# Two routed expert layers on one core: where GpSimd rounds the second weights, and how the second layer's token lists are made

## The chip, the cores and the metric

The kernel runs on one core of a Trainium2 chip. The metric is the device time of one execution in microseconds (us); three executions of the kernel before took 448.25, 448.32 and 449.85 us, median 448.32 us. In the profile TensorE's matmuls are called PE and its weight loads PEld, VectorE is DVE, ScalarE is ACT, GpSimd is POOL, and SyncE, which only issues transfers here, is SP.

## The reference

```python
attn_out = _attn_ref(x, state)            # 4 x 8 x (512 + 32) x 64
x = attn_out.transpose(0, 2, 1, 3).reshape(2176, 512)
x = _moe_ref(x, w_gate, w1, w2, capacity) # 8 experts, capacity 576, top 1
return _moe2_ref(x, w_gate, w1, w2)       # 8 experts, no capacity

# an expert layer, in short:
expert = argmax(x @ w_gate); gate = softmax(x @ w_gate)[expert]
h = relu(x_e @ w1[e])                     # 512 -> 1024
y = h @ w2[e]                             # 1024 -> 512
out[token] = gate * y                     # zero for a token beyond the capacity
```

## The kernel before

The attention comes first, then the two expert layers, called layer 0 and layer 1 (`L` in the code). Within a layer the tokens of each expert are taken in groups of 512, a "stage" each (`stage(L, k)`, L1472, and `tail`, L1527): tokens are gathered by an indirect DMA, turned by TensorE, multiplied by the first weights, passed through the relu and multiplied by the second weights. Each float32 product is made of three products of rounded parts, high by high, high by low and low by high. So every weight has to be split. The high part is a cast on ACT. The low part is weight minus high part, one subtraction on GpSimd or VectorE. Here three stages run in layer 0 and three in layer 1.

**Order of a stage.** A stage is 16 products in a fixed order (`ORDER`, L1455): eight first products (`m1_quad`, L1159, three steps of four matmuls each) and eight second products (`m2_quad`, L1171, four steps of three matmuls each), the second product of a chunk one place behind the first product of the next. These are 56 steps, numbered from 0. Every engine gets its instructions in the order in which the program is written. After each step the program puts in other work (`Part.__call__`, L1504): first one advance of a foreground generator, then the events listed for that step number, then some advances of background work (`tick`). `yield` in a generator means "the rest goes behind the next step". What the foreground generator has not done by the end of its part of the stage (in layer 0's stages 1 and 2 that is step 31) is written out at once, with no product between.

**Splitting the second weights.** `wsplit(1, c, on)` (L275) splits a quarter `c` of the second weights: ACT casts 128x1024 elements (L280), and POOL, or DVE where `on` says 0, subtracts (L281). Four quarters are done behind the steps `SPLIT2`. Steps 1, 3, 5, 7 (`SPLITB`) split the second half of the first weights the same way in tiles of 128x512 (L1385). A quarter `c` is first needed by the second product `2c`, that is at steps 6, 20, 34 and 48. Behind the last split stands `load_next`, which has SP load the next stage's second weights into the same raw buffers.

**Routing of layer 1.** While layer 0's stages 1 and 2 and layer 1's stage 0 run, the outputs of the stage before are routed for layer 1. `Logits` turns 128-token tiles on TensorE and multiplies them by the gate weights (L1221, L1231, L1232). When the last tile's logits are there, `behind` (L1245) runs as the foreground generator: the expert by maximum and comparisons on DVE (`argmax_onehot`, L284, which yields after every third operation), then the "rank products" on TensorE that count earlier tokens of the same expert (L1260 to L1264), then place and gate of each token on DVE (`slots`, `gate_of`), the row stores by indirect DMA on POOL (`stores`, L1193), and then for each tile two one-hot matrices on DVE (`enlist`, L339 and L341) and two "list products" on TensorE that write token numbers into expert lists in PSUM (`enlist_mm`, L347). The one-hots have two buffers, used in turn, and the list product of a tile is written two steps behind its one-hots. In layer 0's stage 2 there follow `set_apart` (L366) and `early_list` (L432), which copies the lists out of PSUM, multiplies them once more (L442) and works out the row numbers for layer 1's first gather (L415). In layer 1's stage 0, `plan_lists` (L575) does the same for all lists (L582, L413), and `planned` (L1594) waits for the plan, has POOL convert it (L1596) and has SP start loading the weights of layer 1's stage 1.

Of the kernel before, what the change touches and what calls it, by code (L numbers as in the profile page):

```python
# [13 lines left out]
F16 = mybir.dt.float16  # L14
# [6 lines left out]
P = 128  # L21
# [13 lines left out]
QT = NEARLY  # L35
NJ = -(-(NTOK + NROWS - 1) // (QT * P)) * QT
NK = E * NJ
# [21 lines left out]
LISTS = (30, 32, 34, 36)  # L59
CUT = (2, 9, 11)  # L60
SPLITA = (0, 2, 4, 6)
SPLITB = (1, 3, 5, 7)
SPLIT2 = (0, 8, 14, 20)
TQ, TQ2, FG, STEP = (3, 2, 1, 3)
PLANNED, READY, GET = ((20, 29), 37, 0)
GAP = 2
HINT0 = 30
TURNS0 = ((0, 1, 2), (4, 5, 6), (6, 7, 8))
ON = ((1, 1, 1, 1), (1, 1, 1, 1), (0, 0, 0, 0), (0, 0, 0), (1, 1, 1, 1))
TURNS = ((6, 7, 8), (8, 10, 12), (12, 13, 14))  # L70
ALL = (ET.Pool, ET.Activation, ET.PE, ET.DVE, ET.SP)
WHY = "the value is a count worked out on the chip within these bounds"
# [3 lines left out]
def moe_kernel(ctx: ExitStack, tc: tile.TileContext, x, state, wg1, w1a, w2a, cap, wg2, w1b, w2b, out):  # L76
# [14 lines left out]
    lists = listp[0:KH, 0:2]  # L91
# [58 lines left out]
    def run_all(g):  # L150
        for _ in g:
            clock[0] += 1
# [119 lines left out]
            k = t.shape[1]  # L272
            SP.dma_start(out=t, in_=src[:, c * k:(c + 1) * k, :])

    def wsplit(which, c, on=ON[2], quick=False):  # L275
        t, h, l = raw[0][which][c], wset[which][0][c], wset[which][1][c]
        if quick:
            DVE.tensor_copy(h, t)
        else:
            ACT.copy(h, t)  # L280
        (POOL if on[c] else DVE).tensor_tensor(out=l, in0=t, in1=h.bitcast(F32), op=ALU.subtract)  # L281
# [55 lines left out]
    def enlist(oc, ov, np_, pp, ek, code, res):  # L337

        DVE.tensor_scalar(oc[0:np_], iofm[0:np_], ek[0:np_], None, op0=ALU.is_equal)  # L339
        yield  # L340
        DVE.tensor_scalar(ov[0:np_], iofb[0:np_], pp[0:np_], code[0:np_], op0=ALU.is_equal, op1=ALU.mult)  # L341
        yield
        res.append((np_, oc, ov))

    def enlist_mm(np_, oc, ov):
        for h in range(2):
            PE.matmul(lists[:, h], oc[0:np_, h * KH:(h + 1) * KH], ov[0:np_], start=False, stop=True, skip_group_check=True)  # L347
# [17 lines left out]
    def set_apart(pool):  # L365

        run = runs_[1]
        t = pool.tile([P, E], F32, tag="sa", name="sa")
        DVE.tensor_scalar(t, run, -1.0, float(NROWS), op0=ALU.mult, op1=ALU.add)
        yield  # L370
        DVE.tensor_scalar(t, t, 0.0, None, op0=ALU.max)
        yield
        DVE.tensor_tensor(out=t, in0=t, in1=first, op=ALU.mult)
        yield
        DVE.tensor_tensor(out=run, in0=run, in1=t, op=ALU.add)
        yield
# [742 lines left out]
    gy = wk2.tile([P, QT + 2], F32, name="gy")  # L1119
    meta = wk2.tile([P, NY, 3], F32, name="meta")  # L1120
    dsti = wk2.tile([P, NY], I32, name="dsti")
    oc2 = wk2.tile([P, 2, NK], F16, name="oc2")
    ov2 = wk2.tile([P, 2, P], F16, name="ov2")
    qs = ctx.enter_context(tc.tile_pool(name="qs", bufs=1, space=bass.MemoryType.PSUM))
    ph = [qs.tile([P, 512], F32, name=f"ph{i}") for i in range(2)]
    py = [qs.tile([P, 512], F32, name=f"py{i}") for i in range(QT)]
# [115 lines left out]
                ev += [(t, lambda i=2 * j + k: self.turn(i)) for k, t in enumerate(ts)]  # L1242
            return ev

    def behind(lt, counted=None):  # L1245


        n, y0, lg = lt.n, lt.y0, lt.lg
        pool = Sized(n)
        m = meta[:, y0:y0 + n]  # L1250
        while lt.done < n:
            yield
        oh = pool.tile([P, n, E], BF16, "oh", "oh2")
        mv = []
        DVE.tensor_copy(dsti[:, y0:y0 + n], m[:, :, 2])
        yield from every(STEP, argmax_onehot(pool, lg, n, m[:, :, 1], oh, mv))

        w = n * E
        ohv = oh.rearrange("p n e -> p (n e)")
        PE.matmul(pyv[:, 0:w], upper, ohv, start=True, stop=True)  # L1260
        for i in range(1, n):
            PE.matmul(pyv[:, i * E:w], ones, ohv[:, 0:(n - i) * E], start=False, stop=True, skip_group_check=True)
        for i in range(n):
            PE.matmul(pyv[:, w:w + E], ones, ohv[:, i * E:(i + 1) * E], start=(i == 0), stop=(i == n - 1))  # L1264
        run = runs_[1]
        pre = pool.tile([P, n, E], F32, "pre", "pre2")
        res = []

        def places():
            DVE.tensor_tensor(out=pre, in0=bc(run[:, None, :], [P, n, E]), in1=pyv[:, 0:w].rearrange("p (n e) -> p n e", n=n), op=ALU.add)  # L1270
            DVE.tensor_tensor(out=run, in0=run, in1=pyv[:, w:w + E], op=ALU.add)
            if counted is not None:
                counted()
            yield
            yield from slots(pool, oh, mv[1], pre, n, res)

        def gates():
            yield from gate_of(pool, lg, mv[0], n, gy[:, 0:n])
            DVE.tensor_copy(ysb[:, y0:y0 + n, DM], gy[:, 0:n])
            stores(0, range(y0, y0 + n))  # L1280

        yield from every(2 * STEP, abreast(places(), gates()))
        todo = []
        for i in range(n):
            run_all(enlist(oc2[:, i % 2], ov2[:, i % 2], P, res[0][:, i:i + 1], res[1][:, i:i + 1], m[:, i, 0:1], todo))
            for _ in range(GAP):
                yield
            if i:
                enlist_mm(*todo.pop(0))
        enlist_mm(*todo.pop(0))  # L1290
        yield

    def nothing(m):

# [65 lines left out]
    def load_next(L, k, *which):  # L1360

        if k < ML:
            n = load_reg(L, 0, spo, ML)
            with tc.If(n > k) as cmp:
                e = load_reg(L, QEXP + k, spo, E - 1)
                for i in which:
                    wload(0, i, W[L][i], e)
            if L == 0 and k > 2:
                with cmp.Else():
                    run_all(load_first(1, which))  # L1370
        elif L == 0:
            run_all(load_first(1, which))
# [20 lines left out]
    def at(places, f, *args):  # L1393
        return [(p, lambda c=c: f(*args, c)) for c, p in enumerate(places)]
# [63 lines left out]
    def hint(label, hints):  # L1458

        with tc.block():  # L1460
            for h, engs in hints:
                tc.mark_branch_hint_location(label, hint=h, engines=engs)
# [8 lines left out]

    def stage(L, k, ev=(), ticks=0, fg=()):  # L1472

        lists = [at(SPLIT2, lambda c: wsplit(1, c, ON[4 if L or k else 2])), ev]
        if L or k:
            lists.append(at(SPLITB, split1, 1))
        if k:
            lists.append([(SPLITB[-1] + 1, lambda: load_next(L, k + 1, 0)), (SPLIT2[-1] + 1, lambda: load_next(L, k + 1, 1))])
        st = Stage(lists)
        DVE.tensor_copy(mcur, cols(L, k))  # L1480
        DVE.tensor_copy(gq[0], gq[1])
        if k == 0:
            st.common(CUT[2], ticks, fg)
            return st
        s = 2 * (k - 1)
        y = 0 if k % 2 == 0 else NY - 1

        def small1(kind):
            yield from one(L, kind - 1, s, y)
            load_small(L, s + 1)  # L1490
            get_small(L, s + 1)

        def small2(kind):
            yield from one(L, kind - 1, s + 1, NY - 2)
            if k < NA:
                load_small(L, 2 * k)
                get_small(L, 2 * k)

        if L == 0:
            if k == 1:  # L1500
                fill_out()
            nothing(meta[:, y:y + 1])
        if k <= NA:
            st.variants(CUT[0], kd_[s], small1)  # L1504
        st.common(CUT[1], 0, fg)
        if L == 0:
            nothing(meta[:, NY - 2:NY - 1])
        if k <= NA:
            st.variants(CUT[2], kd_[s + 1], small2, f"end{L}{k}", hints(L, k))
        else:  # L1510
            st.common(CUT[2])
        return st

    def beside(L, k, lt):

        if L == 0:
            yield from behind(lt)
            if k == 1:
                yield from popular(rp, 1, runs_[1], most)
            if k == 2:  # L1520
                yield from apart()

    def apart():
        yield from set_apart(rp)
        yield from early_list(rp, 1)
# [66 lines left out]
    def planned(L):  # L1592
        while "nr" not in rt:
            assert bgq  # L1594
            tick()
        POOL.tensor_copy(ri[L], rt.pop("nr"))  # L1596
        load_next(L, 1, 0)
# [18 lines left out]
        x_quad(t, ysb[:, 1 + t], py[t], False)  # L1616
    reads[3][2]()
    bgq.append(chain(fills(2, 3), route(1, B - 1, (3, 0, 0, 0), False, (plan_runs(rp, 0), chain(positions(0), until_placed(), positions(1)))), enlist_all()))
    st = stage(0, 0, at(LISTS, list_product) + [(LISTS[-1] + 1, listed), (PLANNED[0], lambda: planned(0)), (SPLIT2[-1] + 1, lambda: load_next(0, 1, 1)), (READY, room), (HINT0, lambda: hint("end00", (("LikelyTaken", ALL),)))], TQ)
    ready(0)  # L1620
    list_clear()
    deeper(st, 0, 0)
# [2 lines left out]
    def routed():  # L1625
        yield from behind(lt, lambda: bgq.append(plan_runs(rp, 1)))
        bgq.append(plan_lists(rp, 1))

    lt = Logits(QT + 2, 0)
    st = stage(1, 0, lt.events(TURNS0) + [(PLANNED[1], lambda: planned(1)), (PLANNED[1] + 1, lambda: load_next(1, 1, 1))], TQ2, routed())  # L1630
    ready(1)
    deeper(st, 1, 0)

# [37 lines left out]
```

## Time and profile before

| | us | share of the span |
|---|---|---|
| median of three runs | 448.32 | |
| profiled execution | 452.34 | |
| its span, first to last instruction | 450.5 | |
| PE busy | 418.6 | 93% |
| PEld busy | 301.6 | 67% |
| DVE busy | 186.3 | 41% |
| POOL busy | 184.8 | 41% |
| ACT busy | 161.3 | 36% |
| mean granted TensorE clock | 0.987 of full | |

The shares are averages over a span in which PE nearly always has work. A row of a timeline reads: start in us, length in us, engine, line, operation, output <- inputs, shape, count, and in brackets how long the engine was idle before it and what ended that wait. Neighbouring matmuls overlap in it, so what a step costs is read from one start to the next and not from the lengths.

Layer 0's stage 1 starts at about 116.4 us of the span, its stage 2 at 188.1, layer 1's stage 0 at 260.7 and its stage 1 at 315.6.

### The profile page before, as it was taken

To read this page: it belongs to the slowest core of one execution; us is meant where nothing else is said; L and a number is where in the kernel's file an instruction comes from. 1 tells how busy PE (TensorE), PEld (TensorE's weight loads), DVE (VectorE), ACT (ScalarE), POOL (GpSimd) and SP (SyncE) were. 2 spreads that over 40 slices of the span, in tenths; PEclk is the share of its full clock that TensorE was granted. 3 is DMA by queue.
4 is the path that set the end of the run, shared out by engine and by line. 5 is a ranking of instruction groups with operands and counts; after the bars stand their busy time and mean duration, and the time that the engine had idled before them with its cause. 6 is when DMAs were issued, how large, how long until landed. Compare 5 with 4: busy or idle time off the path is not lost. (4 is left out here: it accounts for less than half of the span.)

```text
span 450.5 us, 8000 instructions
## 1 busy us (share of the span) xinstructions
PE 418.6 (93%) x2746; PEld 301.6 (67%) x2746; DVE 186.3 (41%) x576; ACT 161.3 (36%) x291; POOL 184.8 (41%) x166
## 2 busy tenths in 40 slices
PE   7899879999998999999988999999989999999991
PEld 4676658867646847757754876788547848768780
DVE  7988898943314511512650336854210101411111
ACT  4587553203443214545202464114313214452110
POOL 7343300017245454064442544475717207677003
PEclk9899999999999999999989999999999999999997
DMA  7965999599999478089331200239989668210002
GB/s 218 304 169 130 353 176 182 98 341 342 384 402 371 177 226 331 3 300 378 120 98 51 73 0 4 101 135 388 387 291 328 228 226 277 75 49 7 9 0 93
DMA packets 48229, 88.13 MB, mean 196 GB/s; under 512 B 8592, under 2 KB 23440, under 8 KB 48144
## 3 DMA queue, kind: packets, MB, share of 16 engines
q1 hardware_dynamic: 43344, 72.43, 50.5%
q0 software_dynamic: 4800, 14.71, 9.3%
q8 instruction: 36, 0.59, 0.6%
q14 instruction: 49, 0.40, 0.3%
HBM read 66.65 MB, written 21.52 MB: 196 GB/s over the span
## 5 line engine op out<-in xcount | busy, mean ns | idle before, releaser
L1157 DVE SCALAR_TENSOR_TENSOR hTl<-ph,hTh 128x512 fp32r<-128x512 f32 x48 | 33.2, 691 | 199.4 <-ACT hTh L1156 184.0
L1175 PE MATMUL py<-w1h,hTh 128*128 128x512 f32 x192 | 81.4, 424 | 0.0
L1175 PE MATMUL py<-w1h,hTl 128*128 128x512 f32 x192 | 75.4, 393 | 0.0
L1175 PE MATMUL py<-w1l,hTh 128*128 128x512 f32 x192 | 75.1, 391 | 0.0
L1156 ACT ACTIVATE hTh<-ph 128x512 fp32r<-128x512 f32 x48 | 28.7, 599 | 128.9 <-PE ph L1165 74.3
L1385 POOL TENSOR_TENSOR w0l<-raw,w0h 128x512 fp32r<-128x512 f32 x40 | 50.9, 1291 | 36.7 <-ACT w0h L1384 34.5
L281 POOL TENSOR_TENSOR w1l<-raw,w1h 128x1024 fp32r<-128x1024 f32 x20 | 47.8, 2397 | 41.3 <-ACT w1h L280 41.2
L1165 PE MATMUL ph<-xTh,w0h 128*128 128x512 f32 x192 | 54.1, 403 | 4.4 <-PEq L1578 2.5
L1165 PE MATMUL ph<-xTl,w0h 128*128 128x512 f32 x192 | 55.6, 411 | 0.1
L1165 PE MATMUL ph<-xTh,w0l 128*128 128x512 f32 x192 | 54.9, 408 | 0.0
L1165 PEld LDWEIGHTS ph<-xTh,w0h 128*128 128x128 f32 x192 | 35.2, 188 | 13.8 <-issue 4.3
L1165 PEld LDWEIGHTS ph<-xTl,w0h 128*128 128x128 f32 x192 | 35.2, 188 | 13.8 <-issue 6.1
L1175 PEld LDWEIGHTS py<-w1h,hTh 128*128 128x128 f32 x192 | 36.1, 188 | 9.5 <-issue 3.4
L1165 PEld LDWEIGHTS ph<-xTh,w0l 128*128 128x128 f32 x192 | 35.3, 191 | 9.8 <-issue 2.5
L1175 PEld LDWEIGHTS py<-w1h,hTl 128*128 128x128 f32 x192 | 36.0, 188 | 8.1
L1175 PEld LDWEIGHTS py<-w1l,hTh 128*128 128x128 f32 x192 | 36.3, 189 | 6.6 <-issue 1.0
L1193 POOL DMA_INDIRECT out_dram<-ysb,dsti x15 | 14.9, 993 | 60.3 <-ACT ysb L1183 53.3
L1193 POOL DMA_INDIRECT yrows<-ysb,dsti x16 | 16.0, 1000 | 27.4 <-DVE oc L339 8.0
L1384 ACT CAST w0h<-raw 128x512 fp32r<-128x512 f32 x40 | 23.8, 617 | 5.4 <-DMA raw<-in_moe_w_dram 5.2
L280 ACT CAST w1h<-raw 128x1024 fp32r<-128x1024 f32 x24 | 25.1, 1046 | 0.1
L977 PE MATMUL pav<-vg,e1T 128*128 128x264 f32 x56 | 16.6, 421 | 1.3 <-ACT lgx L982 1.3
L1324 PE MATMUL pyT<-raw,xTf 128*32 128x256 f32 (+1 forms) x144 | 16.8, 454 | 0.0
(355 smaller groups left out, 555.0 us busy)
## 6 DMA issues: line engine op xcount, KB each, us to landing
raw<-in_moe_w_dram SPq DMA_DIRECT2D x104, 512.0 KB
out_dram<-zb SPq DMA_DIRECT2D x2, 2176.0 KB
xb<-in_x_dram SPq DMA_DIRECT2D x6, 512.0 KB
xrows<-xr SPq DMA_DIRECT2D x8, 256.0 KB
yrows<-zb SPq DMA_DIRECT2D x3, 514.0 KB
yrows<-zb SPq DMA_DIRECT2D x3, 512.0 KB
xb<-in_x_dram SPq DMA_DIRECT2D x4, 256.0 KB
xrows<-ysb SPq DMA_DIRECT2D x4, 256.0 KB
```

What stands on the lines that cost most here:

```text
L280: ACT.copy(h, t)
L281: (POOL if on[c] else DVE).tensor_tensor(out=l, in0=t, in1=h.bitcast(F32), op=ALU.subtract)
L977: PE.matmul(pv[:, a, 0:GW], e1_[b][:, r % 2, a, r // 2], vg[:, b, a], start=True, stop=True)
L1156: ACT.activation(out=hTh[:, c % 2], in_=p, func=AF.Relu)
L1157: DVE.scalar_tensor_tensor(out=hTl[:, c % 2], in0=p, scalar=0.0, in1=hTh[:, c % 2].bitcast(F32), op0=ALU.max, op1=ALU.subtract)
L1165: PE.matmul(p, w[k][:, 0, c * P:(c + 1) * P], u[:, k], start=(i == 0 and k == 0), stop=(i == 2 and k == NC1 - 1))
L1175: PE.matmul(py[t], u[:, c % 2, t * P:(t + 1) * P], w[c // 2][:, c % 2], start=(c == 0 and i == 0), stop=(c == NC2 - 1 and i == 2))
L1193: i = POOL.indirect_dma_start(out=(yrows if L == 0 else out)[:, :], out_offset=bass.IndirectOffsetOnAxis(ap=dsti[:, y:y + 1], axis=0), in_ ...
L1324: PE.matmul(pyv[q * n:(q + 1) * n, 0:w], xTf[:, c, 0:n], w1[c][:, 0, q * w:(q + 1) * w], start=(c == 0), stop=(c == NC1 - 1))
L1384: ACT.copy(h, t)
L1385: (POOL if ON[half][c] else DVE).tensor_tensor(out=l, in0=t, in1=h.bitcast(F32), op=ALU.subtract)
```

## The change

The places and the engine of the second weights' splits now differ by stage. Layer 0's stage 0 and layer 1's stages 1 and 2 keep theirs. In layer 0's stages 1 and 2 the quarters 2 and 3 go from steps 14 and 20 to steps 11 and 31, still on POOL. In layer 1's stage 0 the four go from steps 0, 8, 14, 20 to 0, 3, 6, 36, and the last goes from POOL to DVE. The load of the next second weights goes with the last split: behind step 32 in place of 21 in layer 0's stages 1 and 2, behind step 37 in place of 30 in layer 1's stage 0.

Each tile of a routing gets its own pair of one-hot buffers. One step is put between the argmax and the rank products. The one-hots are made one tile a step (two tiles a step in layer 0's stage 2), then a few steps pass (four; in layer 0's stage 2 three, in which `set_apart` is done), and then all list products are written in one place.

```diff
-SPLIT2 = (0, 8, 14, 20)
+SPLIT2 = {(0, 0): (0, 8, 14, 20), (1, 0): (0, 3, 6, 36), 0: (0, 8, 11, 31), 1: (0, 8, 14, 20)}
-GAP = 2
-ON = ((1, 1, 1, 1), (1, 1, 1, 1), (0, 0, 0, 0), (0, 0, 0), (1, 1, 1, 1))
+ON = ((1, 1, 1, 1), (1, 1, 1, 1))
+ON2 = {(0, 0): (0, 0, 0, 0), (1, 0): (1, 1, 1, 0), 0: (1, 1, 1, 1), 1: (1, 1, 1, 1)}
...
-    oc2 = wk2.tile([P, 2, NK], F16, name="oc2")
-    ov2 = wk2.tile([P, 2, P], F16, name="ov2")
+    oc2 = wk2.tile([P, QT + 2, NK], F16, name="oc2")
+    ov2 = wk2.tile([P, QT + 2, P], F16, name="ov2")
...
-    def behind(lt, counted=None):
+    def behind(lt, counted=None, per=1, gap=4, between=()):
...
         yield from every(STEP, argmax_onehot(pool, lg, n, m[:, :, 1], oh, mv))
-
+        yield
...
         for i in range(n):
-            run_all(enlist(oc2[:, i % 2], ov2[:, i % 2], P, res[0][:, i:i + 1], res[1][:, i:i + 1], m[:, i, 0:1], todo))
-            for _ in range(GAP):
+            run_all(enlist(oc2[:, i], ov2[:, i], P, res[0][:, i:i + 1], res[1][:, i:i + 1], m[:, i, 0:1], todo))
+            if i % per == per - 1:
                 yield
-            if i:
-                enlist_mm(*todo.pop(0))
-        enlist_mm(*todo.pop(0))
-        yield
+        between = iter(between)
+        for _ in range(gap):
+            next(between, None)
+            next(between, None)
+            yield
+        run_all(between)
+        for u in todo:
+            enlist_mm(*u)
...
-        lists = [at(SPLIT2, lambda c: wsplit(1, c, ON[4 if L or k else 2])), ev]
+        sp, on = ((d[(L, k)] if (L, k) in d else d[L]) for d in (SPLIT2, ON2))
+        lists = [at(sp, lambda c: wsplit(1, c, on)), ev]
...
-            lists.append([(SPLITB[-1] + 1, lambda: load_next(L, k + 1, 0)), (SPLIT2[-1] + 1, lambda: load_next(L, k + 1, 1))])
+            lists.append([(SPLITB[-1] + 1, lambda: load_next(L, k + 1, 0)), (sp[-1] + 1, lambda: load_next(L, k + 1, 1))])
...
         if L == 0:
-            yield from behind(lt)
+            if k == 2:
+                yield from behind(lt, None, 2, 3, set_apart(rp))
+                yield from every(STEP, early_list(rp, 1))
+            else:
+                yield from behind(lt)
             if k == 1:
                 yield from popular(rp, 1, runs_[1], most)
-            if k == 2:
-                yield from apart()
...
-    st = stage(1, 0, lt.events(TURNS0) + [(PLANNED[1], lambda: planned(1)), (PLANNED[1] + 1, lambda: load_next(1, 1, 1))], TQ2, routed())
+    st = stage(1, 0, lt.events(TURNS0) + [(PLANNED[1], lambda: planned(1)), (SPLIT2[(1, 0)][-1] + 1, lambda: load_next(1, 1, 1))], TQ2, routed())
```

## Rows read from the trace of the kernel before

**Rows 1.** The page: two costly groups (count | busy us, mean ns | idle before).
```profile
L1157 DVE SCALAR_TENSOR_TENSOR hTl<-ph,hTh 128x512 fp32r<-128x512 f32 x48 | 33.2, 691 | 199.4 <-ACT hTh L1156 184.0
...
L280 ACT CAST w1h<-raw 128x1024 fp32r<-128x1024 f32 x24 | 25.1, 1046 | 0.1
```

**Rows 2.** PE's waits over the span: us in total, times, longest us.
```profile
PE pyT L1260 <- DVE oh L299: 2.6, 3, 1.4
...
PE pyT L1308 <- DMA raw<-in_moe_w_dram: 0.3, 1, 0.3
```

**Rows 3.** Timeline of PE around the rank products of the three routings.
```profile
145.43 0.18 PE L1260 MATMUL pyT<-oh,upper 128*128 128x32 bf16 x1 [1.43 <-DVE oh L299]
...
213.90 1.09 PE L1165 MATMUL ph<-xTh,w0h 128*128 128x512 f32 x4
214.82 1.10 PE L1165 MATMUL ph<-xTh,w0l 128*128 128x512 f32 x4
216.21 0.18 PE L1260 MATMUL pyT<-oh,upper 128*128 128x48 bf16 x1 [0.29 <-DVE oh L299]
...
216.51 1.17 PE L1165 MATMUL ph<-xTl,w0h 128*128 128x512 f32 x4
217.52 0.40 PE L1175 MATMUL py<-w1h,hTh 128*128 128x512 f32 x1
...
218.21 0.39 PE L1175 MATMUL py<-w1h,hTh 128*128 128x512 f32 x1
...
278.30 0.18 PE L1260 MATMUL pyT<-oh,upper 128*128 128x48 bf16 x1 [0.91 <-DVE oh L299]
```

**Rows 4.** Timeline of PE, end of the routing in layer 0's stage 2.
```profile
227.63 0.27 PE L347 MATMUL listp<-ov,oc 128*96 128x128 f16 x2 [0.91 <-DVE ov L341]
228.79 0.61 PE L442 MATMUL pyT<-elm,la 96*128 96x4 f32 x4 [0.89 <-DVE elm L437]
229.80 1.53 PE L1165 MATMUL ph<-xTh,w0h 128*128 128x512 f32 x4 [0.41 <-issue]
```

**Rows 5.** Windows (length, busy of PE, PEld, DVE, ACT, POOL; then granted clock, DMA).
```profile
230.47:233.88 3.41, 3.41 (x15) 2.26 (x17) 2.85 (x6) 0.59 (x1) 2.52 (x2) 0.50 0.10 39
```

**Rows 6.** Timeline of PE: four list products in one place, layer 1's stage 0.
```profile
290.43 0.39 PE L347 MATMUL listp<-ov,oc 128*96 128x128 f16 x4
290.63 0.48 PE L1175 MATMUL py<-w1h,hTh 128*128 128x512 f32 x1
```

**Rows 7.** Source line L290: count, ns min/median/max, first and last start.
```profile
L290 DVE TENSOR_TENSOR rt<-lg,rm x3: 2186/2264/2311, 142.2 to 275.1; 128x48 f32<-128x48 f32 x2, 128x32 f32<-128x32 f32 x1
L290 DVE TENSOR_TENSOR rt<-lgs,rm x2: 200/241/282, 35.9 to 68.8; 128x40 f32<-128x40 f32 x1, 128x120 f32<-128x120 f32 x1
```

**Rows 8.** Timeline of DVE: argmax and one-hots in stage 2, lists in layer 1's stage 0.
```profile
213.06 2.19 DVE L290 TENSOR_TENSOR rt<-lg,rm 128x48 f32<-128x48 f32 x1
...
219.64 0.27 DVE L339 TENSOR_SCALAR oc<-iofm,rek 128x192 f16<-128x192 f16 x1
...
220.05 0.27 DVE L339 TENSOR_SCALAR oc<-iofm,rek 128x192 f16<-128x192 f16 x1
...
293.61 4.09 DVE L413 TENSOR_TENSOR sel<-sel,plu 128x52 f32<-128x52 f32 x1
```

**Rows 9.** Timeline of POOL: splits of second weights, stores and the plan.
```profile
212.78 2.40 POOL L281 TENSOR_TENSOR w1l<-raw,w1h 128x1024 fp32r<-128x1024 f32 x1 [5.24 <-ACT w1h L280]
...
229.62 0.97 POOL L1193 DMA_INDIRECT yrows<-ysb,dsti  x1 [3.39 <-PE pyT L442]
230.60 2.39 POOL L281 TENSOR_TENSOR w1l<-raw,w1h 128x1024 fp32r<-128x1024 f32 x1
...
292.83 4.79 POOL L281 TENSOR_TENSOR w1l<-raw,w1h 128x1024 fp32r<-128x1024 f32 x2
297.54 0.22 POOL L1596 CAST ri<-nr 128x28 int32<-128x28 f32 x1
```

**Rows 10.** Timeline of ACT before step 12's relu, layer 0's stage 2.
```profile
208.56 0.60 ACT L1156 ACTIVATE hTh<-ph 128x512 fp32r<-128x512 f32 x1 [1.21 <-PE ph L1165]
```

More of the change, by code (lines that the diff above doesn't have):

```diff
@@ L273, in wload, with wsplit @@
             SP.dma_start(out=t, in_=src[:, c * k:(c + 1) * k, :])
-    def wsplit(which, c, on=ON[2], quick=False):
+    def wsplit(which, c, on=(0, 0, 0, 0), quick=False):
         t, h, l = raw[0][which][c], wset[which][0][c], wset[which][1][c]
@@ L1618, in moe_kernel @@
     bgq.append(chain(fills(2, 3), route(1, B - 1, (3, 0, 0, 0), False, (plan_runs(rp, 0), chain(positions(0), until_placed(), positions(1)))), enlist_all()))
-    st = stage(0, 0, at(LISTS, list_product) + [(LISTS[-1] + 1, listed), (PLANNED[0], lambda: planned(0)), (SPLIT2[-1] + 1, lambda: load_next(0, 1, 1)), (READY, room), (HINT0, lambda: hint("end00", (("LikelyTaken", ALL),)))], TQ)
+    st = stage(0, 0, at(LISTS, list_product) + [(LISTS[-1] + 1, listed), (PLANNED[0], lambda: planned(0)), (SPLIT2[(0, 0)][-1] + 1, lambda: load_next(0, 1, 1)), (READY, room), (HINT0, lambda: hint("end00", (("LikelyTaken", ALL),)))], TQ)
     ready(0)
```

## The prediction

> **What bounds the kernel now.** By the table above PE is busy in 93% of the span, so I read PE's waits first: whatever PE does not wait for is off the path as long as it stays covered. The longest is three waits, 2.6 us together, of the rank products for the argmax's last result on DVE [rows 2]. I then went to PE's timeline at the three routings. The reader should see 1.43, 0.29 and 0.91 us of idle time ahead of the rank products [rows 3] and, where layer 0's stage 2 runs out of steps, idle stretches of 0.91, 0.89 and 0.41 us within some 3 us, with only tiny products between [rows 4]. Windows show the price of the latter: the granted clock is 0.50 for 3.41 us right behind them, that is 1.2 GHz where it is 2.4 GHz otherwise, and PE is busy all that time [rows 5].
>
> Why is the argmax late? Source line L290 tells: on small tiles it takes 2.19 to 2.31 us in the three routings of layer 1 and 0.20 to 0.28 us in the two of layer 0 [rows 7]. In time, the slow one of stage 2 lies at 213.06 to 215.25, and POOL's subtraction of a quarter of the second weights at 212.78 to 215.18 [rows 8, 9]: the DVE operation ends when POOL's does. The same happens at 293.61, a DVE operation of 4.09 us that ends with two POOL quarters, 292.83 to 297.62 [rows 8, 9]. The relu's DVE part, on far larger tiles, has its plain mean of 691 ns [rows 1], so not every DVE operation is held.
>
> **The change, part by part.** Prices of steps first: a first-product step is 0.92 us (213.90 to 214.82), a second-product step 0.69 (217.52 to 218.21) [rows 3].
>
> *Argmax and rank products.* The lock costs 2.19 - 0.2 = 2.0 us in each routing [rows 7, 8], and the added step gives 0.69 to 0.92 us more. In layer 0's stages the quarter of step 14 goes to step 11, at least 2.3 us earlier (0.92 + 2 x 0.69), against its 2.40 us on POOL [rows 9]. In stage 2, where the argmax starts behind step 14, that frees it. In stage 1 it starts behind step 12, and I expect some 0.6 us of overlap to remain. The margin there is 2.0 - 0.6 + 0.69 = 2.1 us against a wait of 1.43. In layer 1's stage 0 the argmax starts behind step 8. POOL now has three quarters and four first-weight tiles in steps 0 to 7 and may run up to 1 us into it, but the rank products stand five steps later, behind step 13. So I take all three waits as gone: 1.43, 0.29 and 0.91 us. ACT has to fit the casts, 1.05 us each [rows 1]; at step 11 it sat idle for 1.21 us before the next relu [rows 10], and at step 6 of layer 1's stage 0 I charge 0.1 us of delay to a tile's turn.
>
> *Lists in layer 0's stage 2.* From the place where step 19 could start (214.82 + 0.92 = 215.74) to step 31 at 229.80 it took 14.06 us [rows 3, 4]. The plain steps in it are 4 x 0.92 + 8 x 0.69 = 9.20. After the change there stand in it the rank products, 0.30 (216.21 to 216.51) [rows 3], twelve list products in one place at 0.05 each (four took 290.43 to 290.63) [rows 6], 0.6, and the product with the copied lists, 0.61 [rows 4]: 10.7, with 0.1 for changes of kind 10.8. That is 3.25 us less, stage 2's 0.29 included. Counting the generator's steps, everything up to L415 is written by step 30, where before half of it was written at once behind step 30. Is DVE in time? The rank products end near 217.0; relu part, places and gates then keep it until about 219.7, and six tiles of one-hots at 0.41 us (219.64 to 220.05) [rows 8] until 222.2. The list products stand behind step 27, at 217.0 + 5 x 0.69 + 3 x 0.92 = 223.2: 1.0 us of cover. If it is gone, PE waits again.
>
> *Clock.* 3.41 us at half the clock with PE busy cost 3.41 x 0.5 = 1.7 us [rows 5]. What PE did before it fell is the row of waits [rows 4]; without them I take the 1.7 as given back. The bounds are 0 and 1.7.
>
> The Trainium skill, in "TensorE: Matmul & The Clock Gate", section "What's actually happening", has the clock at half by default, with activity releasing it and idleness of the array bringing it back. By that rule short waits with products between them need not be what brought it down, and the 1.7 us would stay lost, at 442.5 us. The trace has the fall right behind the waits and no fall behind the single wait of 1.43, so I give the rule a rival of its own below.
>
> *Layer 1's stage 0.* The two quarters that stood on POOL behind the last store (292.83, 4.79 us) no longer hold the plan's conversion at 297.54 [rows 9], so the loads for the next stage start up to 4.8 us sooner, and the 0.33 us that PE waited for such a load go [rows 2]. Quarter 3 costs DVE one subtraction at step 36 where PE needs it at step 48: 0. SP's second load goes behind it, seven steps later in the program; but SP is held by buffers and not by steps, and the buffer is free about when the plan is. I take 0.33 gained; if that cover fails, SP's queue, with the small experts' weights behind, is later by up to seven steps' 5 us less the 4.8 gained.
>
> *No cost or gain.* Quarter 3 in layer 0's stages moves to step 31, but in stage 2 it already ran behind the last store (230.60, written at step 20) [rows 9], as POOL works in order. So the raw buffer is freed as before, and SP's loads with it. Regrouping the list products of the other two routings saves changes of kind, 0.48 against 0.39 us for the next product [rows 3, 6]: 0 to 0.3 each, taken as 0. The extra buffers cost nothing on an engine.
>
> The sum: 1.43 + 3.25 + 1.7 + 0.91 + 0.33 - 0.1 = 7.5 us. Made against the profiled execution, 452.34 us (span 450.5 and 1.8 around it), this gives 444.8. The timed runs' median is 4.0 us lower, 448.3; taking the same waits to be in it, 440.8 us.
>
> **Rivals.**
> - *The clock still falls.* For it: the list products come in a lump, and twelve tiny products use little of the array. Against: no wait is left beside them. 448.3 - 7.5 + 1.7 = 442.5 us.
> - *One lump waits.* In layer 0's stage 2 two tiles' one-hots a step are too much for DVE, PE waits for the last one as before, 0.91 + 0.89 [rows 4], and the clock falls, 1.7: 3.5 us lost, 444.3. For it: the cover is only 1.0 us. Against: the one-hots no longer wait for list products to free a buffer.
> - *The change doesn't do what it says.* The moved quarters are late on ACT or POOL and still lie under the argmax. Then the lock's 2.0 us stay, the added step takes 0.69 of each wait (0.69 + 0.29 + 0.69 = 1.7 us), and stage 2's end is as before: 446.6. For it: ACT does the casts between other work. Against: its idle 1.21 us.
> - *Slower: every lump waits.* All list products of a routing now stand behind its last one-hot, so one late one-hot stalls them all. If DVE is behind in all three routings, by the 1.8 us seen in stage 2, and the clock falls each time, that is 3 x (1.8 + 1.7) = 10.5: 448.3 - 7.5 + 10.5 = 451.3 us. It decides from 7.5 / 3 = 2.5 us a lump, so from a wait of 0.8 us with the clock's fall. For it: in layer 1's stage 0 DVE also works out the plan in these steps. Against: four steps, at least 2.8 us, pass in which no one-hot is added.
>
> **How the numbers follow.** Forecast 440.8 at 0.60; clock 442.5 at 0.16; one lump 444.3 at 0.12; not as it says 446.6 at 0.07; slower 451.3 at 0.05. The range goes down to the forecast less the regroupings (0.6) and half of the three runs' spread of 1.6 us, 0.8, so 439.4, and up to the one-lump case plus 0.8, 445.1, which leaves out the last two. A measurement of this kernel tells 0.5%, 2.2 us, from no change. The first three cases are faster by more than that, 0.88; the fourth is within it, 0.07; the last is slower, 0.05.
>
> **What would show it.** In the changed kernel's profile L290 should be near 0.2 us in stage 2 and in layer 1's stage 0, and under 1 us in stage 1. PE's waits should no longer list L1260, L347 or L442, step 31 of stage 2 should come some 4.7 us earlier, counting stage 1's 1.4, and the granted clock stay at 1.00 there. L1596 should run right behind the last store. The prediction is wrong if a wait for a one-hot stands ahead of L347, if the clock falls at another place, or if a split or load behind step 31 or 36 holds PE.

## The result

| | before | after |
|---|---|---|
| median of six runs each, us | 448.31 (447.79 to 449.99) | 442.03 (440.14 to 443.12) |
| profiled execution, us | 452.34 | 443.12 |
| its span, us | 450.5 | 441.3 |
| mean granted clock in it | 0.987 | 0.990 |

The ratio is 0.985, 95% interval 0.982 to 0.988, that is 6.3 us less. The profiled execution of before is 4.0 us above its median, so the two profiles lie further apart, by 9.2 us. A second measurement of the changed kernel, in another session (e8 below), gave 0.983 (0.980 to 0.985).

**PE's waits after the change** (us in total, times, longest us). The rank products [rows 2] are gone from the list, and so is the wait for the small experts' weights. A new one has come, the product with the copied lists (L582):

```profile
PE ph L1165 <- ACTq L1585: 1.6, 1, 1.6
...
PE pyT L582 <- DVE la L579: 1.2, 1, 1.2
```

**Source line L290** (count, ns min/median/max, first and last start). The argmax's operation that took 2.19 to 2.31 us [rows 7] has its plain length:

```profile
L290 DVE TENSOR_TENSOR rt<-lg,rm x3: 193/207/209, 142.3 to 267.9; 128x48 f32<-128x48 f32 x2, 128x32 f32<-128x32 f32 x1
```

**Timeline of PE, end of the routing in layer 0's stage 2.** Twelve list products in a row, then the product with the copied lists, no idle time anywhere, and step 31 at 224.36, which was 229.80 [rows 4]:

```profile
220.88 0.39 PE L1175 MATMUL py<-w1h,hTl 128*128 128x512 f32 x1
221.10 0.83 PE L347 MATMUL listp<-ov,oc 128*96 128x128 f16 x12
221.75 0.48 PE L1175 MATMUL py<-w1h,hTh 128*128 128x512 f32 x1
...
223.22 0.50 PE L442 MATMUL pyT<-elm,la 96*128 96x4 f32 x4
...
224.36 0.63 PE L1165 MATMUL ph<-xTh,w0h 128*128 128x512 f32 x2
```

**Timeline of DVE** before them: the last one-hot ends at 220.31, so the list products, written behind it, had 0.8 us of cover:

```profile
217.54 0.27 DVE L339 TENSOR_SCALAR oc<-iofm,rek 128x192 f16<-128x192 f16 x1
...
219.74 0.57 DVE L341 TENSOR_SCALAR ov<-iofb,rpp,meta 128x128 f16<-128x128 f16 x1
```

**Windows** (length; busy of PE, PEld, DVE, ACT, POOL; granted clock, DMA share, GB/s): the clock is 1.00 there, where it was 0.50 for 3.41 us [rows 5].

```profile
218.00:224.40 6.40, 6.40 (x41) 5.33 (x40) 4.66 (x23) 0.60 (x1) 4.91 (x5) 1.00 0.45 169
224.40:237.60 13.20, 11.65 (x82) 6.46 (x80) 0.64 (x8) 3.57 (x6) 4.46 (x3) 1.00 0.26 87
```

**Timeline of PE, layer 1's stage 0.** The rank products no longer wait, but the product with the copied lists does, 1.17 us:

```profile
270.53 0.20 PE L1260 MATMUL pyT<-oh,upper 128*128 128x48 bf16 x1
...
280.38 0.83 PE L347 MATMUL listp<-ov,oc 128*96 128x128 f16 x12
281.02 1.18 PE L1165 MATMUL ph<-xTl,w0h 128*128 128x512 f32 x4
283.37 0.65 PE L582 MATMUL pyT<-mk,la 96*128 96x52 f32 x4 [1.17 <-DVE la L579]
```

DVE's timeline and a window of its work between the two show why. Behind the argmax's last operation, which ends at 269.00, DVE's next one is its part of a relu, and it stands 1.66 us for ACT's part of it. Then (third number after the length in the window) it is busy for 11.30 of 11.70 us with the plan and the one-hots, and the copy is its next operation.

```profile
268.79 0.21 DVE L299 TENSOR_TENSOR oh<-desc,rv 128x48 bf16<-128x48 f32 x1
270.67 0.69 DVE L1157 SCALAR_TENSOR_TENSOR hTl<-ph,hTh 128x512 fp32r<-128x512 f32 x1 [1.66 <-ACT hTh L1156]
271.27 0.19 DVE L1270 TENSOR_TENSOR pre<-run,pyT 128x48 f32<-128x48 f32 x1
...
282.90 0.41 DVE L579 COPY la<-listp 96x256 f32<-96x256 f32 x1
```

```profile
271.20:282.90 11.70, 11.00 (x57) 8.71 (x55) 11.30 (x80) 1.44 (x4) 5.06 (x5) 1.00 0.26 98
```

**Timeline of POOL there:** the plan's conversion (now L1603) stands right behind the last store, at 284.77 where it was 297.54 [rows 9].

```profile
283.81 0.98 POOL L1193 DMA_INDIRECT yrows<-ysb,dsti  x1 [3.82 <-DMA yrows<-ysb,dsti]
284.77 0.24 POOL L1603 CAST ri<-nr 128x28 int32<-128x28 f32 x1
```

By stages, from the starts of the first products in the two profiled executions, the 9.2 us of span go to: everything ahead of layer 0's stage 1, which the change hardly touches, -0.5 (it takes 113.7 to 116.4 us in the twelve profiles); stage 1 -1.71; stage 2 -5.20; layer 1's stage 0 -0.39, its stage 1 -0.59, its stage 2 -0.83. The last isn't the change's work either, as far as I can name an edit: 0.80 of it is a wait for a small expert's output that some profiles have and others not (e4 below has it, e7, which differs by two pauses in layer 1's stage 0, has not).

### The profile page after: what moved, and what is told of

The parts are those of the page before. It is cut to its first block, busy times and chain, and to the rows that moved or that the text cites. A ratio compares the mean times of both kernels' runs of the same rounds, so it can differ in the third digit from the quotient of the medians.

```text
span 441.3 us, 7992 instructions
## 1 busy us (share of the span) xinstructions
PE 414.7 (94%) x2746; PEld 301.3 (68%) x2746; DVE 172.9 (39%) x577; ACT 161.1 (36%) x291; POOL 182.4 (41%) x165
## 5 line engine op out<-in xcount | busy, mean ns | idle before, releaser
L281 POOL TENSOR_TENSOR w1l<-raw,w1h 128x1024 fp32r<-128x1024 f32 x19 | 45.4, 2392 | 36.5 <-ACT w1h L280 36.3
L1165 PE MATMUL ph<-xTh,w0l 128*128 128x512 f32 x192 | 53.8, 402 | 0.0
```

Of the source, the lines that this page charges most:

```text
L1165: PE.matmul(p, w[k][:, 0, c * P:(c + 1) * P], u[:, k], start=(i == 0 and k == 0), stop=(i == 2 and k == NC1 - 1))
```

## The experiments

All were timed in five rounds beside the kernel before. They stood in three sessions (e1 to e4, e5 to e8, e9 and e10), in which the kernel before had medians of 450.15, 449.43 and 451.52 us; so it is ratios that are compared. One thing more is read from the runs. Each execution has a mean granted clock; span times (1 - clock) is what the clock fell short of full, and the rest of the span is listed beside it. Not all of the shortfall costs time. In each of the twelve profiles the clock goes to half 2 to 5 us behind PE's last product, and 2.5 to 3.9 us of the shortfall stand there, where PE has no work; in before it is 2.5 us, 9.63 x (1 - 0.74):

```profile
440.87:450.50 9.63, 0.00 (x0) 0.00 (x0) 0.75 (x1) 0.04 (x1) 2.94 (x3) 0.74 0.28 109
```

So the two columns are read by their differences between kernels only, and a difference has this spread in it. Means with standard errors:

| kernel | runs | ratio, 95% | short of the full clock, us | rest of the span, us |
|---|---|---|---|---|
| before, three sessions | 41 | | 4.7 ± 0.2 | 443.6 ± 0.2 |
| after, two sessions | 11 | 0.983 to 0.985 | 3.4 ± 0.3 | 436.8 ± 0.3 |
| e1, splits alone | 8 | 0.992 (0.989 to 0.995) | 5.0 ± 0.6 | 440.1 ± 0.3 |
| e5, list order alone | 6 | 0.990 (0.988 to 0.993) | 3.1 ± 0.3 | 440.3 ± 0.4 |
| e3, step alone | 12 | 1.001 (0.998 to 1.003) | 5.8 ± 0.5 | 442.5 ± 0.5 |
| e2, splits put back | 6 | 0.990 (0.987 to 0.993) | 3.9 ± 0.4 | 439.9 ± 0.5 |
| e6, step taken out | 6 | 0.987 (0.984 to 0.990) | 4.3 ± 0.5 | 437.6 ± 0.2 |
| e4, one pause more | 6 | 0.983 (0.980 to 0.986) | 3.6 ± 0.4 | 437.2 ± 0.3 |
| e7, three pauses more | 5 | 0.979 (0.976 to 0.982) | 3.8 ± 0.5 | 434.8 ± 0.6 |

### Splits alone (e1)

```diff
 before.py
-SPLIT2 = (0, 8, 14, 20)
+SPLIT2 = {(0, 0): (0, 8, 14, 20), (1, 0): (0, 3, 6, 36), 0: (0, 8, 11, 31), 1: (0, 8, 14, 20)}
+ON2 = ...   # and the loads behind the last split, as in the change
```

> The kernel before with the new places of the splits alone (with the loads behind them); lists and rank products as before. My theory (two separate causes): the three waits of the rank products (1.43, 0.29, 0.91 us) and the 0.33 us for a load go, but stage 2 of layer 0 still ends with waits of 0.9 and 0.9 us for one-hots and copied lists and a clock of 0.50 for 3.41 us: 2.9 us faster than before, 445.4 us, ratio 0.9935. Rival A (the lock is all: with POOL out of the way the one-hots come in time too): waits and fall of the clock go as well, about 441 us, ratio 0.984. Rival B (the added step and the lump are all): 447.5 us or slower.

Measured 446.30 us, ratio 0.992. In the profile the rank products' waits are gone without the added step (1.47, 0.44 and 1.04 us less at the three places), but stage 2's end is as it was, and its clock worse. PE's waits (us in total, times, longest) and the windows behind them; lines are one higher here:

```profile
PE listp L348 <- DVE ov L342: 1.5, 2, 1.0
...
PE pyT L443 <- DVE elm L438: 0.9, 1, 0.9
```

```profile
220.00:226.90 6.90, 5.15 (x29) 3.97 (x27) 3.09 (x14) 0.60 (x1) 3.47 (x4) 1.00 0.44 161
226.95:233.78 6.83, 6.72 (x28) 4.75 (x32) 1.35 (x13) 1.53 (x2) 2.12 (x2) 0.50 0.07 24
```

PE is idle for 1.75 of 6.90 us in the first window, and for 6.83 us behind it the clock is at half. The splits do not touch this part of the gain.

### Splits put back (e2)

```diff
 after.py
-SPLIT2 = {(0, 0): (0, 8, 14, 20), (1, 0): (0, 3, 6, 36), 0: (0, 8, 11, 31), 1: (0, 8, 14, 20)}
+SPLIT2 = {(0, 0): (0, 8, 14, 20), 0: (0, 8, 14, 20), 1: (0, 8, 14, 20)}   # all on POOL; load at the old place
```

> The changed kernel with the splits where they were before (and loads as before): lists a buffer per tile and the added step alone. My theory: the lock stays (L290 2.2 us three times), the added step takes 0.69 of the waits of 1.43 and 0.91 and all of 0.29, stage 2 gains 2.96 and the clock's 1.7, and the 1.2 us that PE now waits for the copied lists in layer 1's stage 0 stay: 5.1 us faster than before, 443.2 us, ratio 0.989, with rank waits of about 0.7 and 0.2 us. Rival A (the lock is all): 447 us or more, one-hots of stage 2 late again. Rival B (step and lump are all): 442.0 us as the changed kernel, no rank wait.

Measured 445.61 us, ratio 0.990, as expected. Stage 2 keeps its gain of 2.81 us and its clock. Of what comes back, 0.7 us lie in layer 0's stage 1, where the rank products wait again (0.5 us), and most lies in layer 1: the two POOL quarters stand between the last store and the plan's conversion again, and PE, now earlier, waits longer for the load that follows from it than it did before (0.3 us [rows 2]). POOL's timeline, then PE's waits:

```profile
284.66 0.97 POOL L1193 DMA_INDIRECT yrows<-ysb,dsti  x1 [4.21 <-PE pyT L582]
285.64 4.78 POOL L281 TENSOR_TENSOR w1l<-raw,w1h 128x1024 fp32r<-128x1024 f32 x2
290.37 0.20 POOL L1603 CAST ri<-nr 128x28 int32<-128x28 f32 x1
```

```profile
PE pyT L1312 <- DMA raw<-in_moe_w_dram: 1.5, 1, 1.5
...
PE pyT L582 <- DVE la L579: 0.9, 1, 0.9
```

Against after, layer 1's stage 1 is 1.8 us longer. So clearing POOL behind the stores is worth 0.6 us on the kernel before (that stage in e1) and 1.8 beside the rest of the change.

### The added step alone (e3)

```diff
 before.py, behind()
         yield from every(STEP, argmax_onehot(pool, lg, n, m[:, :, 1], oh, mv))
-
+        yield
```

> The kernel before with one empty step ahead of the rank products alone. My theory: rank waits 0.7, 0 and 0.2 us, 1.7 us faster by that, but stage 2 has one step less for its lists, so one tile more is left for the end: 0 to 0.6 us given back; 446.6 to 447.2 us, ratio 0.996 to 0.9975, the clock at 0.50 behind stage 2's step 30 as before. Rival B: the waits are gone whole, 445.7 us.

Measured 450.13 us, ratio 1.001 (0.998 to 1.003): the expected 1.1 to 1.7 us are not seen in the time. In the profile they are there: the rank products' waits fall from 2.6 to 0.7 us, and layer 0's stage 1, its stage 2 up to step 31 and layer 1's stage 0 are 1.5 us shorter together (-0.91, -0.91, +0.29). By the table the rest of the span is 1.1 us shorter than before, and the clock falls short by 1.1 us more. With standard errors of 0.5 each, and 1.2 us more of the shortfall behind PE's last product in e3's profile than in before's (3.7 and 2.5), that is no more than a hint. Why the times do not show the gain stays open.

### List order of stage 2 alone (e5)

```diff
 before.py, beside(); behind() takes the new order only where `between` is given; a buffer per tile
-            yield from behind(lt)
...
+            if k == 2:
+                yield from behind(lt, None, 2, 3, set_apart(rp))
+                yield from every(STEP, early_list(rp, 1))
```

> The kernel before with one part of the change alone: the second stage of layer 0 makes its one-hots two tiles a step into a buffer per tile, works out the plan's start beside them, and issues the six pairs of list products together. Splits and rank products stay in their old places. Theory (two causes beside each other, list order and splits): the list products go close together, step 31 of stage 2 comes some 2.8 us earlier, the clock has no fall at that stage's end (another 1.7 to 2.0 us); the rank-product waits stay at about 2.6 us, and layer 1's stage 0 has no longer a wait for the copied lists than the kernel before, since its rank products still come late. Ratio 0.990 to 0.991. Rival (the lists lose their waits only because the rank products and the splits are out of GpSimd's and VectorE's way): the list products, now in one lump, wait for the last one-hot by 1 to 3 us, the clock falls as before, ratio 0.996 to 1.000.

Measured 445.09 us, ratio 0.990. Stage 2 is 4.65 us shorter, the rank products wait as before, and there is no wait for L582. Its windows (from 224 on) and PE's waits:

```profile
224.00:240.00 16.00, 14.42 (x93) 8.72 (x92) 1.15 (x8) 3.73 (x7) 5.67 (x5) 1.00 0.25 73
```

```profile
PE pyT L1260 <- DVE oh L299: 2.6, 3, 1.4
```

The list order by itself takes out both the waits and, on the mean of its runs, 1.6 ± 0.4 us of the clock's shortfall. PE, earlier here too, waits 0.8 us for the load behind layer 1's plan, where it waited 0.3 us before. e1 and e5 add up: 0.8% and 1.0% against the whole change's 1.5 to 1.8%.

### The step taken out (e6)

```diff
 after.py, behind()
         yield from every(STEP, argmax_onehot(pool, lg, n, m[:, :, 1], oh, mv))
-        yield
+
```

> The changed kernel without the one step that was put ahead of the rank products. Theory (the moved splits have already taken VectorE's hold away, as the run with the splits alone showed with rank-product waits of 1.47, 0.44 and 1.04 us gone and no step): the rank products wait 0.3 us at one place (stage 1 of layer 0: 1.77 gained with the step, 1.47 without), and in layer 1's stage 0 the plan starts a step earlier, so that TensorE's wait for the copied lists falls from 1.17 us to 0.6 or less. Within 0.5 us of the changed kernel on the same chip, ratio to the kernel before 0.983 to 0.987. Rival (the step is what hides the rank one-hots): the three waits come back with 1.4, 0.3 and 0.9 us, the time is 2 us above the changed kernel, ratio 0.988 to 0.990.

Measured 443.79 us, ratio 0.987; the changed kernel beside it had 442.26. Neither expectation came true. The rank products' waits do not come back; stage 1 loses 0.1 us, not 0.3 (the expected 1.77 against 1.47 was counted to a step that has the rank products ahead of it in one kernel and behind it in the other). But the wait for the copied lists grew and did not shrink:

```profile
282.21 0.65 PE L582 MATMUL pyT<-mk,la 96*128 96x52 f32 x4 [2.16 <-DVE la L579]
```

Counted from the stage's start, PE gets to that product 0.9 us sooner than in after, a step, and the copy comes 0.1 us later. The rank products, 0.7 us sooner here, don't move DVE's plan: the relu part ahead of it waits for ACT as in after, and the plan's first operation (L1270) stands 18.01 us into the stage in both.

```profile
269.42 0.69 DVE L1157 SCALAR_TENSOR_TENSOR hTl<-ph,hTh 128x512 fp32r<-128x512 f32 x1 [1.67 <-ACT hTh L1156]
270.02 0.19 DVE L1270 TENSOR_TENSOR pre<-run,pyT 128x48 f32<-128x48 f32 x1
```

### One pause, three pauses, and three without the step (e4, e7, e9, e10)

```diff
 after.py, plan_lists()
         DVE.tensor_copy(la, lists)
         yield PAUSE
+        yield PAUSE      # e4: one; e7 and e10: three; e9: four, and no step ahead of the rank products
```

> The changed kernel with one more pause in the plan of layer 1's lists, so that the product with the copied lists (L582) is written a step later. My theory of what the changed kernel lost against the forecast: DVE works through plan and one-hots without a break until the copy at 282.90, and PE waits 1.17 us for that copy; a step of 0.69 us later the wait is 0.3 to 0.5 us, 0.7 to 0.9 us faster than the changed kernel, about 441.2 us. Rival: the wait only moves, because the next relu's part on DVE (hTl) is late by the same backlog: no change against 442.0 us and a wait of about 1 us at a second product.

Measured 442.39 us, ratio 0.983. The wait fell from 1.17 to 0.5 us, and layer 1's stage 0 was 0.7 us shorter. The time does not show it: the ratio is that of the changed kernel.

> The changed kernel with three more pauses between the copy of the lists and the product that reads them (plan_lists). One pause took the wait for the copy in layer 1's stage 0 from 1.17 to 0.5 us. Theory (the product was issued sooner than VectorE, busy without a break for 12 us, could copy): no wait for the copied lists is left, that stage gains 1.2 us against the changed kernel, nothing comes late behind it; time 0.8 to 1.2 us below the changed kernel on the same chip. Rival (the lists are needed right behind): the gathers of stage 1 go out later, and TensorE waits there for rows or for the small experts' input by as much; same time as the changed kernel, or 0.5 us more.

Measured 440.22 us, ratio 0.979 (0.976 to 0.982), against 442.26 and 0.983 (0.980 to 0.985) for the changed kernel on the same chip. The wait is gone and nothing is late behind it: layer 1's stage 0 is 1.43 us shorter than in after, stage 1 the same. PE's timeline:

```profile
283.02 0.40 PE L1178 MATMUL py<-w1h,hTl 128*128 128x512 f32 x1
283.25 0.55 PE L585 MATMUL pyT<-mk,la 96*128 96x52 f32 x4
283.62 0.47 PE L1178 MATMUL py<-w1h,hTh 128*128 128x512 f32 x1
```

> The changed kernel without the step ahead of the rank products, and with four more pauses between the copy of the lists and their product. Without the step alone the wait for the copied lists had grown from 1.2 to 2.2 us and the time by 1.5 us. Theory (the step was worth that only because it put the product that reads the copied lists one step later; with the product put later directly, the step is worth the 0.3 us of stage 1 at most): no wait for the copied lists, rank products as in the run without the step, time within 0.6 us of the kernel with three pauses and the step. Rival (the step itself takes load off VectorE there, whatever follows): 1.2 us or more above the kernel with three pauses and the step.

> The changed kernel with three more pauses once more, on the same chip as the one without the step. Both theories: ratio to the kernel before 0.976 to 0.982; no wait for the copied lists.

Measured on one chip: 441.34 us without the step (ratio 0.980, 0.976 to 0.985), 441.44 with it (0.980, 0.975 to 0.984). With the product put later directly, the step is worth nothing that can be measured; in the profile it is 0.1 us, in stage 1. With three pauses the kernel comes out ahead of both: 2.0 and 2.1% against before in its two measurements, where the changed kernel had 1.5 and 1.8. The intervals of the two overlap, so that the 1.4 us between them rest on the profiles' stage more than on the times.

### The changed kernel again (e8)

> The changed kernel as it is, on the same chip as the other three, to compare them with. Both theories: ratio 0.985 (0.982 to 0.988); the profile shows again no wait for rank products, a wait of about 1.2 us for the copied lists in layer 1's stage 0, and the clock at 1.00 at the end of layer 0's stage 2. The places at which the small expert's copy of its output came 0.8 us late in some profiles and not in others (the second small expert of layer 0's stage 1, the first of layer 1's stage 2) may differ: what one execution shows there is not of the change.

Measured 442.26 us, ratio 0.983 (0.980 to 0.985). The waits are those of the first profile, with one difference. At the end of layer 0's stage 2 the clock fell in this execution, behind the branch at which the program asks whether a further stage is needed (in `deeper`). PE's timeline and the windows:

```profile
234.21 0.40 PE L1175 MATMUL py<-w1h,hTl 128*128 128x512 f32 x1
236.49 1.20 PE L1165 MATMUL ph<-xTh,w0h 128*128 128x512 f32 x4 [1.88 <-ACTq L1585]
```

```profile
234.00:237.84 3.84, 1.96 (x9) 1.30 (x8) 0.54 (x1) 1.11 (x2) 1.02 (x2) 0.99 0.02 6
237.84:241.25 3.41, 3.41 (x10) 2.67 (x9) 0.15 (x1) 0.25 (x1) 2.80 (x3) 0.51 0.55 169
```

The steps in it take 1.6 us longer than in after. So the clock term isn't a sure gain: the change took away one place at which the clock fell, and it can still fall at another, 15 us behind step 31. A third place lies outside the change: in the profiles of before, after and e1 the clock is 0.72 on the mean from 18 to 24 us, in the attention, 1.7 us in each of the three, and 1.00 in the other nine.

## Why the prediction was right, and where it was not

- **Time.** Forecast 440.8, range 439.4 to 445.1; measured 442.03. 6.3 us of the expected 7.5 came. By the table the mean over all runs is 1.3 ± 0.3 us less short of the full clock and 6.8 ± 0.3 less besides, across sessions that differ by up to 1.3 us in the kernel before (its mean in them is 450.2 us, its median beside the first measurement 448.3). That the sum came so near is in part luck. By the stages of the two profiles stage 1 gained 1.71 where 1.43 was forecast, stage 2 with its clock 5.20 (4.95), layer 1's stage 0 0.39 (0.81) and its stage 1 0.59 (0.33): three terms too small and one too large.
- **Argmax and rank products: right.** The hold is gone from L290 at all three places and all three waits with it. In stage 1, 0.6 us of it remains as forecast, on another operation: the cast ahead of the argmax takes 0.84 us and ends with POOL's quarter. What was not seen is that the moved splits and the step do the same thing twice: e1 and e3 each take most of the waits away alone.

DVE's timeline there, and then POOL's quarter:

```profile
141.37 0.84 DVE L1255 CAST dsti<-meta 128x4 int32<-128x4 f32 x1
142.12 0.17 DVE L287 TENSOR_REDUCE rm<-lg 128x4 f32<-128x32 f32 x1
142.32 0.19 DVE L290 TENSOR_TENSOR rt<-lg,rm 128x32 f32<-128x32 f32 x1
```

```profile
139.78 2.39 POOL L281 TENSOR_TENSOR w1l<-raw,w1h 128x1024 fp32r<-128x1024 f32 x1 [0.82 <-ACT w1h L280]
```

- **Lists in layer 0's stage 2: right in size.** Forecast 3.25 us, in the profile 0.42 + 2.81 = 3.23. The cover was 0.8 us, forecast 1.0. e5 shows that it is the list order's own, e1 that the splits have no part in it. Of the two rivals for this place, the lump that waits did not come.
- **Clock: right in sign, too large.** The forecast of 1.7 us was the price of one fall in one profiled execution. The list order takes that fall away (the profiles of before, e1 and e3 have it, those of all kernels with the new order not). The mean over the runs is 1.3 us less all the same. The fall behind the branch in e8 is one reason that a profile shows; in that execution the clock fell at another place, which the prediction names as a sign of being wrong. How often it comes stays open, since the timed runs give a mean clock only.
- **Layer 1's stage 0: the failed step.** "So I take all three waits as gone: 1.43, 0.29 and 0.91 us" was true of the third wait, but its 0.91 us did not stay gained. Behind the rank products PE was 1.0 us ahead; the rest of the stage, with the regrouped list products (taken as 0), gave some 0.5; and then PE stood 1.17 us for the copied lists. The stage gained 0.39. The step counted PE's time and the argmax's, and not what DVE does behind it. Counted from the stage's start, the argmax ends at 15.74 us, where it was 17.58, but DVE then waits for the relu, and its plan starts at 18.01, where it was 18.11; in before the relu's part followed the argmax without a wait:

```profile
278.04 0.21 DVE L299 TENSOR_TENSOR oh<-desc,rv 128x48 bf16<-128x48 f32 x1
278.16 0.68 DVE L1157 SCALAR_TENSOR_TENSOR hTl<-ph,hTh 128x512 fp32r<-128x512 f32 x1
278.78 0.20 DVE L1270 TENSOR_TENSOR pre<-run,pyT 128x48 f32<-128x48 f32 x1
```

  From there the plan and the one-hots keep DVE for 11.6 us, until the copy at 29.64 (0.41 us; it was at 31.26). That is 1.6 us sooner. PE is ready for the product that reads it 2.8 us sooner, at 28.94, where the product started at 31.72: beside the 1.0 us, the new list order has that product behind step 26 of the stage, where it stood behind step 28. The prediction counted neither the two steps nor DVE's late start. It named DVE's plan as what speaks for its slower rival ("in layer 1's stage 0 DVE also works out the plan in these steps"), but looked for the wait at L347; it came one step later, at L582, and with no fall of the clock. e4 and e7 show it by putting the product later, behind steps 27 and 29; e6 by putting it earlier, behind step 25.
- **The wait for a load: right, mis-sized.** Forecast 0.33, 0.59 in the profile. e2 shows that it would have grown to 1.5 had the splits stayed, and in e5 it grew to 0.8.
- **Quarter 3 at step 31, the larger buffers: no cost seen,** as forecast; the quarter runs behind the last store as before (228.39, behind the store of 227.42).

## What to carry to other kernels

When a wait is removed, the engine that was waited for has not become faster: follow it to its next product, ask what it has to take ahead of that and what those operations wait for, and whether that product is now the first to be late. Try to put the consumer later directly (three pauses, 1.4 us in that stage) before moving the producers; and when work is regrouped, look which consumers move up with them. A fall of the clock in one profile is one draw; price it by the mean clock of many runs, and leave out what falls behind the last product.

## What the runs showed of the hardware

- A small DVE operation on SBUF can be held until a POOL subtraction ends: 4.09 us for one of 0.21, through two quarters in a row [rows 8, 9], 3.00 us for one of 0.17 (L415, at 230.03 before and 224.36 after), and 0.84 to 0.99 us for a cast of 0.13. The Trainium skill, in "SBUF — State Buffer", section "Who interferes with whom", has it that a vector operation with two SBUF inputs contends with GpSimd's reads, that a cast can, in a two-port mode, and that a reduction does not. The trace agrees: L290 and L413 have two inputs there and are 0.2 us long with no quarter beside them, and a reduction (L287) is 0.20 us long beside the quarter that holds L290, at 212.82 in before. DVE's timeline in after, layer 1's stage 0:

```profile
266.74 0.99 DVE L1255 CAST dsti<-meta 128x6 int32<-128x6 f32 x1
267.64 0.19 DVE L287 TENSOR_REDUCE rm<-lg 128x6 f32<-128x48 f32 x1
267.87 0.21 DVE L290 TENSOR_TENSOR rt<-lg,rm 128x48 f32<-128x48 f32 x1
...
284.57 0.21 DVE L413 TENSOR_TENSOR sel<-sel,plu 128x52 f32<-128x52 f32 x1
```

- Tiny products with waits between them went with a fall of the clock (0.50 for 3.41 us before, for 6.83 in e1), and the same number of products in one lump did not (1.00 in after and e5). This is what went together, not a rule: in e8 the clock fell behind a single wait of 1.88 us, and in e2 it stayed at 1.00 behind one of 2.02 us at the same place.
- PE stands 1.3 to 2.0 us at that branch in layer 0's stage 2 in all twelve profiles; with three pauses it is the longest wait left behind the attention.
